# Full-height transposes of the half-height attention tiles, and a larger constant in the planner's matmul time

## The chip, the core and the metric

One core of a Trainium2 chip runs the kernel. The metric is the device time of one execution in microseconds (us), taken as the median of several runs. Names of engines are those of the profile: PE is the matrix engine (TensorE), PEld its weight loads, DVE the vector engine, ACT the scalar engine, POOL GpSimd, and SP the queue from which the DMAs are issued.

## What is computed

Attention with a forget gate for 4 batches of 8 heads, 576 rows and 64 columns each, and then two MLPs on its 2304 rows of 512 values, with 2048 hidden units each. All is float32.

```python
scores = scale * np.matmul(q, k.transpose(0, 1, 3, 2))
cum = np.cumsum(np.log(np.clip(f, 0.0001, 1.0)), axis=-1)
scores = np.where(causal, -1e9, scores + cum[:, :, :, None] - cum[:, :, None, :])
attn = np.exp(scores - np.max(scores, axis=-1, keepdims=True))
attn = attn / (np.sum(attn, axis=-1, keepdims=True) + 1e-09)
x = rows(np.matmul(attn, v))               # (2304, 512)
h = x @ w_in;  x = np.maximum(0.01 * h, h) @ w_out
h = x @ w_in2; out = (np.maximum(h, 0.0) + alpha * np.minimum(h, 0.0)) @ w_out2
```

## The kernel before

**Work and stages.** A float32 operand of most products is carried as two float32r parts, hi and lo, and a product is three products of parts. The two MLPs go over 9 blocks of `T` = 256 rows each. A block of the first MLP is 16 chunks of 128 hidden units: `moe_h` multiplies into a chunk (L522, 12 matmuls of 256 columns) and `moe1_y` out of it (L591, 12 of 256 columns). The second MLP does the same with L522 and, in `moe2_y`, L642 (6 matmuls of 512 columns a chunk). The weights come as float64 and are rebuilt on ACT, POOL and DVE while the first block of each MLP runs; some of the first MLP's are then streamed from DRAM for each block (`ws`).

**Attention** is laid out in eight groups, group 0 and group 1 of each batch in turn (`ORDER`). A group 0 holds query rows 0 to 319, a group 1 rows 320 to 575. Every group is done head by head, and a head in query windows of 128 rows (`UNITS`). Group 0 has three windows, which start at rows 0, 128 and 192; of the last only the lower 64 rows count, since the upper 64 belong to the window before (`nq` = 64, `p0 = P - nq` = 64). Scores (L881, with a mask by L886 for the first heads) go to a PSUM bank, DVE adds the decay (L895), ACT takes the exponential (L906), DVE adds and inverts the row sum (L762, L767), and L921 or L923 multiplies the row tile `t` by it. Then `attention_weights` transposes `t` key tile by key tile on PE (L938) into the PSUM tile `tp`, ACT or DVE copies that into `pt` as the hi part (L361 or L363, called from `p_hi`), and DVE subtracts for the lo part (`p_lo`, L952). The product with v is L785 for the first two groups, whose operands stay float32 (`native`), and L795 for the others.

For the window with 64 rows, L938 reads rows 64 to 127 of `t` alone, against the 64x64 lower corner of the identity, and writes 64 columns for each of its three key tiles. All other windows are transposed with 128 rows against the whole identity.

**The order of the work** on all engines is written out ahead by `Plan.run`, a list scheduler that works when the kernel is built. Each operation comes with an engine (or several to choose from), an expected time and a due time; each engine takes the one that is due first among those whose operands and ring slots are free. DMAs are one such engine. The expected time of a matmul is `t_mm(n)` = `max(n / 2.4 + 2.5, 109)` ns for `n` columns, and that of a float32 product of four passes is `t_mm4(n)`. [...] `t_mm` also sets the due times: `span` of a block is 16 chunks x 24 products x `t_mm(256)`, plus 15 us (`ATT_NS`) while attention is left, except that the first block has 60 us. A group's attention is due from `LEAD` = 10 us ahead of a block on; the activations of a chunk are due 8 us (`URGENT`) and the streamed weights 10 us (`AHEAD`) before the product that needs them. On the chip the engines follow the order of the plan, and wait on semaphores for each other, not for the planned times.

Of the kernel before, what the change touches and what calls it, by code (L numbers as in the profile page):

```python
# [62 lines left out]
class Buf:  # L63
    """One tile of a ring; it is allocated when its first operation is emitted."""
# [7 lines left out]
class Ring:  # L72
    """Slots for tiles of a kind, taken in the order of the program, or by whoever comes first."""

    def __init__(self, bufs, make, after=None, ordered=True):
        self.make, self.after, self.ordered = make, after, ordered
        self.made = self.taken = 0
        self.free = [(0, None, i) for i in range(bufs)]  # when and by which engine a slot was left
# [9 lines left out]
class Plan:  # L88
    """List scheduling: operations are given with engine, expected time, due
    time and the buffers they touch; each engine takes the one that is due  # L90
    first among those whose operands and slots are there. They are emitted in
    the order of their start."""
# [4 lines left out]
    @staticmethod  # L97
    def latency(a, b):
        """Expected time between the end of an operation and its user's start."""
        if "dma" in (a, b):  # L100
            return 1000 * (a == "dma") + 1250 * (b == "dma")
        return (0 if a == "pe" else 125) if a == b else 260 if b == "pe" else 200 if a == "pe" else 170

    def op(self, times, due, fn, r=(), w=(), a=(), after=(), hold=(), shared=False, busy=1.0):
        """times: engine -> ns for the engines that may take it, the usual one first; r: read,
        w: written, a: written in a part of its own, hold: only allocated, shared: whether DVE
        takes the SBUF ports that it shares with GpSimd, busy: how busy the PE is with it."""
# [19 lines left out]
    def run(self):  # L127
# [11 lines left out]
        ports = 0  # when the ports that DVE and GpSimd share are free  # L139

        def slots(o, eng, now):
            """When the slots that o has to take are there, or None."""
# [14 lines left out]
        def cost(o, eng, now):  # L157
            """When o would be done on an engine, with a price on the shared ports."""
# [9 lines left out]
        def better(o, eng, now):  # L168
            """Whether no other engine is a better place for o."""
# [13 lines left out]
        while events:  # L183
# [7 lines left out]
            for eng, queue in queues.items():  # L191
                if free.get(eng, 0) > now:
                    continue
                for n in [n for _, n in queue]:
# [17 lines left out]
                    if eng == "pe":  # L212
                        # the array's clock is halved after a tick with few columns
# [31 lines left out]
# Expected times in ns for n columns.  # L245
def t_mm(n, passes=1):
    return passes * max(n / 2.4 + 2.5, 109)
# [43 lines left out]
def tile_forgetting_attention_two_moe(ctx: ExitStack, tc, qk0, qk1, v0, v1, fg, w1, w2, alphaT, out):  # L291
    """Causal softmax attention with a forget-gate decay, then two leaky MLPs.

    Every float32 operand of a matrix product is carried as two float32r parts
    of 12 significant bits, hi + lo, whose sum is exactly the operand.
    """
# [7 lines left out]
    # Each chunk of weights, 128 hidden units, comes in two halves: into and out  # L304
    # of them. Some halves of the first MLP's stay on chip, the others are kept
    # in DRAM once they are converted; some of the second's are converted ahead
    # and kept there too.
# [5 lines left out]
    # ---------------------------------------------------------------- groups  # L313
    # Query windows of 128 rows: (first row, rows that count from the end,
    # first key whose decay comes from the masked copy, key tiles). Key tiles
    # are windows of 128 keys too; where they overlap, v has zeros once.
    # Each group: queries, key tiles with the query they count from, and the
    # row whose cum is the origin of the decay.
# [17 lines left out]
    # Due times in ns: the first MLP's blocks of T rows follow the prologue, and  # L336
    # each group's attention is due during the block before the one it belongs to.
# [10 lines left out]
    # ----------------------------------------------------------------- pools  # L348
# [30 lines left out]
    # PSUM: some banks hold the blocks' outputs.  # L379
# [37 lines left out]
    # what the plan has to know of them  # L417
# [4 lines left out]
    # ------------------------------------------------------------- weights  # L422
    # The weights come as float64: pairs of words, the low one first. The high
    # word taken as a float32 and scaled by 2**-112 has its exponent rebased for
    # float32 (what underflows there becomes zero); shifted by three bits, with
    # the sign put back and the low word's top bits behind, it is the weight.
    w_t = {}

    def slot(which, f, half):
        """The second MLP's weights first take what is new on chip, then what the first leaves."""  # L430
# [8 lines left out]
    def weight(which, f, halves, d):  # L439
        """Load a part of a chunk of an MLP's weights and split it, due at d."""  # L440
# [58 lines left out]
    # ----------------------------------------------------------------- moe  # L499
# [8 lines left out]
    def moe_h(bi, f0, hp=None):  # L508
        """Two chunks of hidden units, which share a bank: product, leaky maximum, split."""
# [70 lines left out]
    def moe1_y(bi, f, g, acc):  # L580
        """Two of the four outputs share a bank, which the first product of the first opens."""
# [51 lines left out]
    def moe2_y(bi, f, g, acc):  # L633
# [17 lines left out]
        if f == NF - 1:  # L651
            parts = 2 if bi == 2 * NB - 1 else 1
            m = DM // parts
            for t in range(T // P):
                osb = new("ysb")
                for c in range(0, DM, m):
# [5 lines left out]
                    for grp in groups:  # L662
                        # the rows of the tile that belong to the group
# [13 lines left out]
    # ----------------------------------------------------------- attention  # L677
    x_raw = {}

    def attention_head(gi, h, d, span):  # L680
        """One head's rows of a group; its units are due from d on over span."""
# [38 lines left out]
        if gi == 0 and h < NBC:  # L720
            # the first heads' sums are broadcast by a product, which is there sooner
# [22 lines left out]
        def pt_ap(s, j0, j1, q0, q1):  # L744
            """Part s of the transposed weights of key tiles j0 to j1. The tiles lie one after
            the other; a last one that only the second window sees has no room for the first."""
# [34 lines left out]
        def pv_native():  # L781
            # v stands beside zeros, so that two heads' products are added in place
# [7 lines left out]
        # The two halves of the product's rows, v's hi and lo parts, are added.  # L790
# [13 lines left out]
        # the blocks that the group's rows belong to: block's tile, its columns, the group's  # L804
# [43 lines left out]
    # The scores are kept negated, without the rows' own cum_i, which cancels in  # L848
    # the softmax; what is added is cum_j less the cum of a row of the group.
# [64 lines left out]
    def attention_weights(g, u, d, t, nm, pt, pt_ap, native):  # L914
# [16 lines left out]
        for j0 in range(0, nb, step):  # L931
# [3 lines left out]
            def transpose(j0=j0, j1=j1, tp=tp):  # L935
                for j in range(j0, j1):
                    k0 = g["kt"][j][0]
                    pe.transpose(tp.ap[:, (j - j0) * nq : (j - j0 + 1) * nq], t.ap[p0:, k0 : k0 + P], ident[p0:, p0:])  # L938

            def parts_of(j0, j1, tp):  # L940
                src = tp.ap[:, : (j1 - j0) * nq]
                if j1 > j0 + 1:
                    src = src.rearrange("p (j q) -> p j q", q=nq)
# [12 lines left out]
            on("pe", (j1 - j0) * (nq / 1.2 + 2), d, transpose, r=[t, ident_b], w=[tp], hold=[pt], busy=nq / 256)  # L956
# [4 lines left out]
    # ------------------------------------------------------------ program  # L961
# [7 lines left out]
    # running sums of the log gates, less those of each group's origin, in two parts  # L969
# [7 lines left out]
    # brings the logarithm's table in  # L977
# [149 lines left out]
```

## Time and profile before

| | |
|---|---|
| time, median of 3 runs | 1046.72 us (1044.7 to 1049.14) |
| span of the profiled execution | 1043.5 us |
| PE busy | 1024.1 us, 98% |
| DVE, ACT, POOL busy | 651.7, 603.6, 85.9 us |
| DMA moved | 166.50 MB |

The time of the profiled execution is not listed apart from the three runs. Its span, from the first to the last instruction, is 3.2 us below their median. A busy time is a union of instructions that overlap in a pipeline, so PE's 98% does not say how fast it works while it is busy; for that one reads the starts of neighbouring groups in the timeline. The first MLP and the attention end at about 640 us, the second MLP fills the rest.

### The profile page before, as it was taken

What the parts mean: (1) busy time and instruction counts of PE and PEld (TensorE: products, weight loads), DVE (VectorE), ACT (ScalarE), POOL (GpSimd) and SP (SyncE); (2) the same over time, 40 slices, a digit from 0 to 9 for tenths busy, and PEclk for the clock granted to TensorE, in tenths of its full rate; (3) what the DMA queues carried; (4) which work ended last, traced back from release to release, by engine and by line L of the source; (5) the groups of instructions that cost most, each with busy time, mean ns of one, the idle gap of its engine ahead of it and who ended that gap; (6) DMA issues with size and microseconds to landing.
All of it is one profiled execution on the core that took longest, in us unless ns stands there. A gap on an engine that the chain in (4) does not pass through costs nothing.

```text
span 1043.5 us, 20123 instructions
## 1 busy us (share of the span) xinstructions
PE 1024.1 (98%) x7466; PEld 964.6 (92%) x7466; DVE 651.7 (62%) x1837; ACT 603.6 (58%) x1354; POOL 85.9 (8%) x159
## 2 busy tenths in 40 slices
PE   7899999999999999999999999999999999999998
PEld 5698999999999999999999999999999999999997
DVE  7799898888887877788885689423222322322322
ACT  7878787767787877887753456334333323323333
POOL 2000221210121111112010001000000000000000
PEclk9999999999999999999999999999999999999999
DMA  8899898576575665767489783001010100000000
GB/s 268 306 311 325 299 308 290 182 255 222 161 257 190 239 217 166 231 229 235 150 280 321 233 311 102 9 33 41 2 41 1 41 21 21 21 2 21 1 21 21
DMA packets 63234, 166.50 MB, mean 160 GB/s; under 512 B 6592, under 2 KB 20320, under 8 KB 63136
## 3 DMA queue, kind: packets, MB, share of 16 engines
q1 hardware_dynamic: 63136, 165.21, 47.2%
q8 instruction: 59, 0.97, 0.4%
q14 instruction: 39, 0.32, 0.1%
HBM read 148.29 MB, written 16.89 MB: 158 GB/s over the span
## 4 chain that ended last, share of the span: by engine, by line
PE 91%; DMA 6%; DVE 2%; ACT 1%; issue 0%; SPq 0%; ACTq 0%; DVEq 0%
PE bank L522 37%; PE bank L642 19%; PE bank L591 18%; PE bank L881 6%; PE bank L938 5%; PE bank L795 4%; PE bank L785 2%; DMA qk<-qk 2%; DMA vr<-v 1%; DMA ws<-wscr 1%; DMA yraw<-yd 1%; DMA raw<-w 1%; DVE g L366 0%; DVE t L895 0%; DVE cv L469 0%
## 5 line engine op out<-in xcount | busy, mean ns | idle before, releaser
L522 PE MATMUL bank<-x,w 128*128 128x256 f32 x1944 | 257.3, 284 | 0.1
L522 PEld LDWEIGHTS bank<-x,w 128*128 128x128 f32 x1944 | 243.7, 191 | 3.6 <-issue 0.4
L546 DVE SCALAR_TENSOR_TENSOR gr<-gr,nalpha,bank 128x256 f32<-128x256 f32 x144 | 62.8, 477 | 213.1 <-ACT bank L539 213.1
L361 ACT ACTIVATE g<-gr 128x512 fp32r<-128x512 f32 x143 | 90.1, 630 | 86.1 <-DVE gr L546 73.9
L366 DVE TENSOR_TENSOR g<-gr,g 128x512 fp32r<-128x512 f32 x144 | 100.6, 699 | 54.3 <-ACT g L361 53.9
L522 PE MATMUL bank<-x,ws 128*128 128x256 f32 x972 | 132.3, 285 | 1.2 <-DMA ws<-wscr 1.2
L536 ACT ACTIVATE gr<-bank 128x512 f32<-128x512 f32 x72 | 43.1, 598 | 154.7 <-PE bank L522 153.8
L642 PE MATMUL bank<-w,g 128*128 128x512 f32 x540 | 132.1, 391 | 0.0
L522 PEld LDWEIGHTS bank<-x,ws 128*128 128x128 f32 x972 | 123.5, 191 | 3.6 <-DMA ws<-wscr 1.7
L591 PE MATMUL bank<-g,ws 128*128 128x256 f32 x864 | 121.7, 288 | 1.3 <-ACT g L361 1.0
L591 PE MATMUL bank<-g,w 128*128 128x256 f32 x864 | 119.7, 286 | 0.0
L642 PEld LDWEIGHTS bank<-w,g 128*128 128x128 f32 x540 | 99.2, 188 | 19.4
L591 PEld LDWEIGHTS bank<-g,ws 128*128 128x128 f32 x864 | 109.5, 191 | 2.8 <-ACT g L361 1.4
L591 PEld LDWEIGHTS bank<-g,w 128*128 128x128 f32 x864 | 109.1, 191 | 0.4 <-issue 0.2
L906 ACT ACTIVATE t<-t,nm 128x128 f32<-128x128 f32 (+4 forms) x160 | 92.6, 580 | 17.2 <-DVE nm L895 16.6
L921 ACT ACTIVATE t<-t,nm 128x128 f32<-128x128 f32 (+4 forms) x139 | 78.2, 574 | 18.9 <-DVE nm L767 17.5
L858 POOL TENSOR_SCALAR_AFFINE_SELECT dm<-cb 128x128 f32<-128x128 f32 (+2 forms) x120 | 59.3, 496 | 358.3 <-DVE nm L895 274.9
L361 ACT ACTIVATE pt<-bank 128x128 fp32r<-128x128 f32 (+4 forms) x189 | 72.0, 408 | 25.9 <-PE bank L938 24.4
L938 PE MATMUL bank<-ident,t 128*128 128x128 f32 (+1 forms) x480 | 73.5, 269 | 1.5 <-ACT t L921 1.3
L952 DVE TENSOR_TENSOR pt<-bank,pt 128x128 fp32r<-128x128 f32 (+1 forms) x144 | 62.4, 452 | 11.7 <-ACT pt L361 10.3
L522 PE MATMUL bank<-x,v 128*128 128x256 f32 x540 | 69.6, 283 | 0.0
L522 PEld LDWEIGHTS bank<-x,v 128*128 128x128 f32 x540 | 68.1, 192 | 1.5
(98 smaller groups left out, 1407.6 us busy)
## 6 DMA issues: line engine op xcount, KB each, us to landing
ws<-wscr SPq DMA_DIRECT2D x112, 512.0 KB, 4.5
raw<-w SPq DMA_DIRECT2D x64, 512.0 KB, 6.3
qk<-qk SPq DMA_DIRECT2D x32, 416.0 KB, 4.4
qk<-qk SPq DMA_DIRECT2D x32, 320.0 KB, 4.5
cb<-cum_d SPq DMA_DIRECT2D x32, 288.0 KB, 4.4
vr<-v SPq DMA_DIRECT2D x16, 480.0 KB, 4.9
wscr<-ws SPq DMA_DIRECT2D x14, 512.0 KB, 5.7
cb<-cum_d SPq DMA_DIRECT2D x31, 160.0 KB, 4.2
```

The lines of the kernel that those rows point to most:

```text
L361: act.activation(out=out, in_=in_, func=AF.Copy)
L366: (dve if e == "dve" else gps).tensor_tensor(out=out, in0=in0, in1=in1, op=ALU.subtract)
L522: pe.matmul(h()[:, f - f0], lhsT=w.ap[:, a, c * P : (c + 1) * P], rhs=x.ap[:, s, c], start=c == 0 and i == 0, stop=c == NC - 1 and i == 2,)
L546: dve.scalar_tensor_tensor(out=gr.ap[:, i], in0=gr.ap[:, i], scalar=nalpha[:, f0 + i : f0 + i + 1], in1=h()[:, i], op0=ALU.mult, op1=ALU.add,)
L591: pe.matmul(acc[c // 2].ap[:, c % 2 * T :][:, :T], lhsT=w.ap[:, a, col : col + P], rhs=g.ap[:, s, at : at + T], start=f == 0 and (a, s) == ...
L642: pe.matmul(acc[t].ap, lhsT=g.ap[:, s, at + t * P : at + (t + 1) * P], rhs=w.ap[:, a], start=f == 0 and (a, s) == (0, 0), stop=f == NF - 1 ...
L858: gps.affine_select(out=dm.ap[:, : nk - split], in_=cb.ap[:, split:nk], pattern=[[-1, nk - split]], compare_op=ALU.is_ge, fill=-MASKED / S ...
L881: pe.matmul(sp_.ap[:, : s1 - s0], lhsT=q.ap[:, ql : ql + P], rhs=k, start=j == 0, stop=j == len(ks) - 1 and not masked,)
L906: act.activation(out=t.ap[:, :nk], in_=t.ap[:, :nk], func=AF.Exp, scale=-1.0, bias=nm.ap[:, last, u : u + 1], accum_out=nm.ap[:, 2, u : u ...
L921: act.activation(out=t.ap[:, :nk], in_=t.ap[:, :nk], func=AF.Copy, scale=nm.ap[:, 3, u : u + 1])
L938: pe.transpose(tp.ap[:, (j - j0) * nq : (j - j0 + 1) * nq], t.ap[p0:, k0 : k0 + P], ident[p0:, p0:])
L952: dve.tensor_tensor(out=lo, in0=src, in1=f32(hi), op=ALU.subtract)
```

## The change

Three lines of the transposes and one of the planner change. The half-height window is transposed like the others, with all 128 rows of `t` and the whole identity, into 128 columns for each key tile; what is copied out of `tp` is the last 64 columns of each. The planner's time for a transpose follows (`P / 1.2 + 2` in place of `nq / 1.2 + 2`, and `busy=0.5`). In `t_mm` the constant is 13.5 ns in place of 2.5 ns, with which all due times after the first block move too. The rest of the diff takes comments out and leaves out a `memset` of zero rows, of which there is none at these sizes.

```diff
 def t_mm(n, passes=1):
-    return passes * max(n / 2.4 + 2.5, 109)
+    return passes * max(n / 2.4 + 13.5, 109)
@@ attention_weights
-                    pe.transpose(tp.ap[:, (j - j0) * nq : (j - j0 + 1) * nq], t.ap[p0:, k0 : k0 + P], ident[p0:, p0:])
+                    pe.transpose(tp.ap[:, (j - j0) * P : (j - j0 + 1) * P], t.ap[:, k0 : k0 + P], ident)
 
             def parts_of(j0, j1, tp):
-                src = tp.ap[:, : (j1 - j0) * nq]
+                src = tp.ap[:, : (j1 - j0) * P]
                 if j1 > j0 + 1:
-                    src = src.rearrange("p (j q) -> p j q", q=nq)
+                    src = src.rearrange("p (j q) -> p j q", q=P)[:, :, p0:]
                 return src, [pt_ap(s, j0, j1, ql + p0, ql + P) for s in range(2)]
@@
-            on("pe", (j1 - j0) * (nq / 1.2 + 2), d, transpose, r=[t, ident_b], w=[tp], hold=[pt], busy=nq / 256)
+            on("pe", (j1 - j0) * (P / 1.2 + 2), d, transpose, r=[t, ident_b], w=[tp], hold=[pt], busy=0.5)
@@
-        on("pool", 100, -9.4e3, lambda i=i, rows=rows: gps.memset(rate[:rows, i : i + 1], -2.0 / SCALE), w=[rate_b])
+        if rows:
+            on("pool", 100, -9.4e3, lambda i=i, rows=rows: gps.memset(rate[:rows, i : i + 1], -2.0 / SCALE), w=[rate_b])
```

## Rows read from the trace of the kernel before

**Rows 1.** The page, part 1: busy us, share of the span, instructions.

```profile
PE 1024.1 (98%) x7466; PEld 964.6 (92%) x7466; DVE 651.7 (62%) x1837; ACT 603.6 (58%) x1354; POOL 85.9 (8%) x159
```

**Rows 2.** The page, part 4: the chain of work that ended last, by engine.

```profile
PE 91%; DMA 6%; DVE 2%; ACT 1%; issue 0%; SPq 0%; ACTq 0%; DVEq 0%
```

**Rows 3.** Windows by stage: length, busy us (instructions) by engine, clock, DMA share.

```profile
0.00:25.00 25.00, 18.99 (x80) 13.88 (x80) 18.17 (x77) 19.07 (x59) 6.66 (x17) 0.93 0.83 269
25.00:125.00 100.00, 94.19 (x635) 83.65 (x636) 89.37 (x265) 80.32 (x191) 6.93 (x10) 1.00 0.92 313
125.00:550.00 425.00, 423.87 (x3487) 416.79 (x3486) 352.65 (x1143) 323.21 (x787) 69.33 (x130) 1.00 0.68 227
550.00:640.00 90.00, 88.03 (x728) 87.22 (x727) 61.58 (x107) 42.66 (x75) 3.00 (x2) 1.00 0.73 254
640.00:1043.50 403.50, 399.00 (x2544) 363.11 (x2542) 129.95 (x250) 138.38 (x246) 0.00 (x0) 1.00 0.07 23
```

**Rows 4.** Groups by form, PE: the two shapes of L938 over the whole span.

```profile
L938 PE MATMUL bank<-ident,t 128*128 128x128 f32 x384 | 60.9, 275 | 1.1 <-ACT t L921 0.9
L938 PE MATMUL bank<-ident,t 64*128 64x64 f32 x96 | 12.9, 242 | 0.4 <-ACT t L921 0.4
```

**Rows 5.** Timeline of PE, a 64-row window: start us, length us, count.

```profile
165.50 1.12 PE L591 MATMUL bank<-g,ws 128*128 128x256 f32 x8
166.55 0.40 PE L938 MATMUL bank<-ident,t 64*128 64x64 f32 x3
166.88 0.74 PE L591 MATMUL bank<-g,ws 128*128 128x256 f32 x4
167.46 1.12 PE L591 MATMUL bank<-g,w 128*128 128x256 f32 x8
```

**Rows 6.** Timeline of PEld, the weight loads of the same stretch.

```profile
165.87 0.55 PEld L591 LDWEIGHTS bank<-g,ws 128*128 128x128 f32 x4
166.55 0.26 PEld L938 LDWEIGHTS bank<-ident,t 64*128 64x128 f32 x3
166.88 0.53 PEld L591 LDWEIGHTS bank<-g,ws 128*128 128x128 f32 x4
```

**Rows 7.** Timeline of PE, three transposes of 128 rows.

```profile
289.82 1.12 PE L591 MATMUL bank<-g,ws 128*128 128x256 f32 x8
290.78 0.49 PE L938 MATMUL bank<-ident,t 128*128 128x128 f32 x3
291.02 1.68 PE L591 MATMUL bank<-g,ws 128*128 128x256 f32 x12
292.54 0.22 PE L881 MATMUL bank<-k,k 128*128 128x128 f32 x1
```

**Rows 8.** Timeline of PE in the second MLP.

```profile
901.62 1.60 PE L522 MATMUL bank<-x,v 128*128 128x256 f32 x12
903.06 1.55 PE L642 MATMUL bank<-ws,g 128*128 128x512 f32 x6
904.44 1.52 PE L642 MATMUL bank<-w,g 128*128 128x512 f32 x6
905.80 4.48 PE L522 MATMUL bank<-x,v 128*128 128x256 f32 x36
```

**Rows 9.** Groups by form, PE, 0 to 60 us: the 64-row transposes.

```profile
L938 PE MATMUL bank<-ident,t 64*128 64x64 f32 x24 | 3.4, 250 | 0.0
```

**Rows 10.** Chain of waits, 0 to 60 us, merged pieces around one window and later.

```profile
32.80 5.22 DMA qk<-qk
...
38.68 0.34 PE bank L938 x3
39.06 0.20 issue
39.27 0.56 ACT t L921
39.84 0.42 DVE t L895
40.27 0.60 DVE cv L469
...
51.51 4.66 DMA vr<-v
```

**Rows 11.** PE's own waits, 0 to 125 us: total us, times, longest.

```profile
PE bank L881 <- DMA qk<-qk: 7.3, 4, 4.4
PE bank L785 <- DMA vr<-v: 2.5, 3, 1.4
```

**Rows 12.** Groups by form: the 192-column copies and subtractions out of PSUM.

```profile
L361 ACT ACTIVATE pt<-bank 128x192 fp32r<-128x192 f32 x24 | 7.9, 330 | 6.4 <-PE bank L938 6.1
L952 DVE TENSOR_TENSOR pt<-bank,pt 128x192 fp32r<-128x192 f32 x24 | 8.5, 353 | 2.8 <-ACT pt L361 2.7
```

**Rows 13.** PE's own waits, 125 to 640 us.

```profile
PE bank L522 <- DMA ws<-wscr: 1.2, 2, 0.9
PE bank L591 <- ACT g L361: 1.0, 2, 0.6
PE bank L938 <- ACT t L921: 0.4, 1, 0.4
PE bank L591 <- DVE g L366: 0.3, 1, 0.3
```

## The prediction

> **What bounds the kernel now.** I read the busy times first [rows 1]: PE is busy for 98% of the span, and nothing else for more than 62%. The chain of work that ended last says the same, 91% of it is PE [rows 2]. Busy is not the same as fast, so next come the windows by stage, for where PE is idle [rows 3]: 6.0 us in the first 25 us (25.00 less 18.99), 5.8 us up to 125 us, 1.1 us of the 425 us up to 550, 2.0 us around the change of the MLPs up to 640, and 4.5 us after it, most of it the tail. The granted clock is 1.00 of 2.4 GHz from 25 us on. So from about 60 us to the end PE is the bound: what is taken off PE's instruction stream there comes off the time one for one, as long as the other engines follow. DVE (352.65 us of 425) and ACT (323.21 us) have 17% and 24% to spare in the longest stage that has attention in it. In the first 60 us it is not PE: the chain changes there between late loads of 4.7 to 5.2 us, DVE and ACT [rows 10], and DMA is busy at 0.83 and 0.92 [rows 3].
>
> How fast PE goes is read from neighbouring starts in the timeline. Twelve products of 256 columns start over 1.44 us (901.62 to 903.06), 120 ns each, and twelve of 512 columns over 2.74 us, 228 ns each [rows 8]. Against 256 / 2.4 = 106.7 ns and 213.3 ns a product has a constant part of 13 to 15 ns.
>
> **The transposes, the part with a price.** There are 96 of 64 rows [rows 4], three for each of the 32 heads' windows of group 0. Take one window amid products that cost 120 ns each. From 165.50 to 167.46 us, 1.96 us, PE does twelve products of L591 and the three transposes [rows 5]: 1.96 - 12 x 0.120 = 0.52 us for the transposes. Where three transposes of 128 rows stand between the same kind of products, from 289.82 to 292.54 us, it does twenty products and the three in 2.72 us [rows 7]: 2.72 - 20 x 0.120 = 0.32 us, or 0.107 us each. The higher transposes are the cheaper ones, by 0.20 us a window; I read 0.19, as starts are rounded to 0.01 us and two are subtracted.
>
> Why this is so can be seen in the loads. The eighth product before the small transposes begins at 165.50 + 7 x 0.12 = 166.34, and the next instruction should begin at 166.46; the first small transpose begins at 166.55. The loads of the products before are all done by 166.42, yet the weight load of the first small transpose begins only with it, at 166.55, and the load of the first product behind them only with that product, at 166.88 [rows 5, 6]. So before the small transposes PE runs empty and loads nothing ahead, 0.09 us, and behind them it does so again. Before the transposes of 128 rows nothing of that is seen: eight products of 0.12 us from 289.82 end at 290.78, where the first transpose begins [rows 7].
>
> The sum: 24 of the 32 windows lie between 125 and 550 us (96 transposes in all [rows 4], 24 of them, eight windows, before 60 us [rows 9]). 24 x 0.19 = 4.6 us, all on the path. The eight early windows have 8 x 0.19 = 1.5 us. One of them is seen on the chain, at 38.68, but what follows it is ACT and then DVE, up to the next late load [rows 10]; PE has gaps there. I count half, 0.7 us, with 0 and 1.5 as ends. Together -5.3 us (-4.6 to -6.1).
>
> **What else the transposes touch costs nothing.** The identity has 128 columns, so each output has 128; three of them are 384 columns and fit the bank. Copy and subtraction still read 192 columns, now with a stride of 128: 330 ns on ACT and 353 ns on DVE today [rows 12]. No row shows the strided read. If it cost half as much again, 24 x (0.17 + 0.18) = 8 us would fall on two engines that have 102 and 72 us to spare in the same 425 us [rows 3]; PE's work hides it. That cover is missing only before 60 us, for eight windows of 0.17 us or 1.4 us at the most. The rows of `t` that are read in addition are written in any case, and no wait is added.
>
> **The planner.** No instruction is added or removed by the constant; it moves the order on all engines and the choice between ACT, DVE and POOL. `t_mm(256)` goes from 109.2 to 120.2 ns and `t_mm(512)` from 215.8 to 226.8, against the 120 and 228 ns of the trace [rows 8]. So the plan had PE 9% too fast in the MLPs and now has it right. The spans of the due times grow from 41.9 to 46.1 us (384 products) plus 15 us. The fixed leads of 10, 10 and 8 us thus become a slightly smaller part of a block. The DMA queue of SP moves with it, all its loads.
>
> The Trainium skill (TensorE: Matmul & The Clock Gate, section Back-to-back issue gap) speaks against this part: it gives N/2.4 + 2.5 ns for the gap, the constant of before. By that page the plan would now be 10% off, by the trace it comes into step; the time of the products on the chip is the same either way, so it bears only on the chances of the two rivals about the order below, and there I go by the trace's 120 ns.
>
> What the new order is worth no row of before shows. It can't win more than PE's idle time that isn't the start or the tail: 5.8 + 1.1 + 2.0 = 8.9 us [rows 3]. Its steady part has nothing to win: of 425 us PE lacks 1.1 us, and all its own waits up to 640 us are 2.9 us in seven pieces [rows 13]. What it can lose is bounded by the nearest rows, late loads before 60 us, at 0.6 to 2 us of PE for a common one (7.3 us in four, 2.5 us in three) and 4.4 us for the worst [rows 11]. I take 0: between a plan that is nearer to the truth and a new order in a stage whose DMA is at 0.92, I see no sign. The ends are -4 us (about half of what is idle) and +7 us (several such loads).
>
> **The sum.** -5.3 us against the span of 1043.5 gives 1038.2 us. The span is 3.2 us below the median of the runs; with that kept, 1046.7 - 5.3 = 1041.4 us. This lies at the edge of the 0.5% (5.2 us, about what a measurement of this kernel can tell from no change), so faster and same split the forecast's chance.
>
> **The rivals.**
> - The order gains too: with PE's times right, loads and conversions before 125 us and at the change of the MLPs come in the order in which PE wants them. Half of 5.8 + 2.0 us, 3.9 us, is won: 1037.5 us. For it: the waits there are for single loads [rows 11, 13]. Against it: DMA is at 0.92 of its time, so a load put earlier puts another one later. 0.22.
> - The order loses a part: one more late load of 4.4 us [rows 11] at the start, 1045.8 us. 0.17.
> - The order loses much, slower than before. The place is the first 125 us. The plan now has PE slower there, so it puts loads of the first weights and of `qk` and `vr` in another order on SP's one queue; every load that is issued behind a wait for a buffer comes late, and PE, which follows a fixed order, stands still. Price: a late load on the chain is 4.7 to 5.2 us [rows 10]. The second such load makes up for the transposes, the third makes it slower: 1041.4 + 3 x 5.2 = 1057 us. 0.08.
> - The transposes don't gain what I say: the gaps around the small ones belong to their place in the program (a wait for `t`) and not to their height. Then the gaps stay and the columns double. By the rows a column of a transpose is 0.107 / 128 us, so 64 more in each of 96 cost at most 96 x 0.053 = 5.1 us: 1051.8 us, still within 0.5%. The same page of the Trainium skill (Back-to-back issue gap) lets the gap grow with the columns, some 60 cycles at 64 and 134 at 128; by it alone, an estimate, 96 x 31 ns = 3.0 us would be added. Against it: transposes of 128 rows wait for the same `t` and show no gap [rows 7]. 0.03.
>
> **How the numbers follow.** The forecast has 0.50, with 1039 to 1044 as its own range; 0.28 of it is below 1041.5, 0.22 above. Faster: 0.28 + 0.22 = 0.50. Same: 0.22 + 0.17 + 0.03 = 0.42. Slower: 0.08. The range reaches down to the gain of order with a little more, 1036 us (-5.3, -4 and 1 us of scatter), and up to the sum with +7 us, 1048.5.
>
> **What would show it.** In the profile after, no 64x64 form of L938 is left and there are 480 of 128x128; twelve to twenty products around three transposes again leave 0.32 us in the timeline; PE's weight loads run ahead into the transposes; PE's busy time from 125 to 550 us becomes shorter for the same work, so that the last L795 comes some 4 us earlier relative to the first. Idle time of PE before 125 us still near 12 us means that the order did nothing; 7 us or less is the first rival, 20 us or more the third. The prediction is wrong if the windows of group 0 don't become shorter by 0.19 us each, or if the first 125 us change by more than the transposes give.

## The result, and the profile after

The changed kernel is slower: 1056.4 us against 1045.7 us (medians of four runs each), a ratio of 1.0099 (95% interval 1.0079 to 1.0120). The forecast was 1041.4 us. Below, "tall" and "small" stand for transposes of 128 and of 64 rows.

The page of the changed kernel, parts 1 and 4 (answers to [rows 1, 2]):

```profile
PE 1027.1 (97%) x7466; PEld 967.1 (92%) x7466; DVE 659.3 (62%) x1842; ACT 603.2 (57%) x1360; POOL 81.2 (8%) x148
...
PE 79%; DVE 8%; DMA 7%; ACT 4%; issue 2%; POOL 0%; ACTq 0%; SPq 0%; DVEq 0%
PE bank L522 33%; PE bank L642 19%; PE bank L591 15%; PE bank L881 4%; PE bank L938 4%; PE bank L795 3%; DMA raw<-w 3%; DMA vr<-v 3%; PE bank L785 2%; DVE g L366 1%; DVE t L895 1%; ACT t L906 1%; DVE pt L952 1%; DVE cv L463 1%; DVE gr L542 1%
```

PE is as busy as before, but only 79% of the chain that ended last is PE, against 91% [rows 2]. DVE has 8% of it where it had 2%, ACT 4% where it had 1%, and loads of raw weights (`raw`) stand on it with 3%. The windows by stage, with the columns of [rows 3], show where:

```profile
0.00:25.00 25.00, 19.40 (x80) 14.50 (x80) 17.75 (x74) 18.48 (x56) 5.77 (x16) 0.93 0.83 267
25.00:125.00 100.00, 90.97 (x611) 80.08 (x610) 89.50 (x261) 78.11 (x188) 4.84 (x7) 1.00 0.91 306
125.00:550.00 425.00, 420.96 (x3437) 413.38 (x3436) 352.24 (x1141) 320.27 (x790) 66.87 (x123) 1.00 0.69 223
550.00:640.00 90.00, 85.50 (x710) 85.07 (x709) 62.04 (x109) 41.04 (x71) 0.76 (x1) 1.00 0.80 275
```

From 25 to 125 us PE begins 611 matmuls where it began 635, from 125 to 550 us 3437 in place of 3487, and 710 in place of 728 after that. The granted clock of these stages is as before. The transposes did what was forecast; groups by form of the changed kernel (answers to [rows 4, 12]):

```profile
L938 PE MATMUL bank<-ident,t 128*128 128x128 f32 x480 | 76.9, 277 | 2.1 <-DVE t L923 1.3 <-ACT t L921 0.4
...
L361 ACT ACTIVATE pt<-bank 128x192 fp32r<-128x192 f32 x24 | 7.8, 325 | 1.1 <-PE bank L938 1.1
...
L952 DVE TENSOR_TENSOR pt<-bank,pt 128x192 fp32r<-128x192 f32 x24 | 8.4, 349 | 0.0
```

All 480 are tall, and the copies and subtractions that now read with a stride take 325 and 349 ns, where they took 330 and 353.

### The profile page after: what moved, and what is told of

Same layout as the page of the kernel before. It is cut to its first block, busy times and chain, and to the rows that moved or that the text cites. A ratio compares the mean times of both kernels' runs of the same rounds, so it can differ in the third digit from the quotient of the medians.

```text
span 1055.0 us, 20133 instructions
## 1 busy us (share of the span) xinstructions
PE 1027.1 (97%) x7466; PEld 967.1 (92%) x7466; DVE 659.3 (62%) x1842; ACT 603.2 (57%) x1360; POOL 81.2 (8%) x148
## 4 chain that ended last, share of the span: by engine, by line
PE 79%; DVE 8%; DMA 7%; ACT 4%; issue 2%; POOL 0%; ACTq 0%; SPq 0%; DVEq 0%
PE bank L522 33%; PE bank L642 19%; PE bank L591 15%; PE bank L881 4%; PE bank L938 4%; PE bank L795 3%; DMA raw<-w 3%; DMA vr<-v 3%; PE bank L785 2%; DVE g L366 1%; DVE t L895 1%; ACT t L906 1%; DVE pt L952 1%; DVE cv L463 1%; DVE gr L542 1%
## 5 line engine op out<-in xcount | busy, mean ns | idle before, releaser
L361 ACT ACTIVATE g<-gr 128x512 fp32r<-128x512 f32 x142 | 89.4, 630 | 96.7 <-DVE gr L546 75.1
L522 PE MATMUL bank<-x,ws 128*128 128x256 f32 x972 | 129.7, 284 | 0.0
L591 PE MATMUL bank<-g,w 128*128 128x256 f32 x864 | 120.2, 288 | 3.5 <-ACT g L361 3.3
L591 PE MATMUL bank<-g,ws 128*128 128x256 f32 x864 | 120.0, 288 | 3.7 <-ACT g L361 3.3
L591 PEld LDWEIGHTS bank<-g,ws 128*128 128x128 f32 x864 | 109.2, 191 | 5.9 <-ACT g L361 4.8
L591 PEld LDWEIGHTS bank<-g,w 128*128 128x128 f32 x864 | 108.9, 191 | 5.4 <-ACT g L361 4.7
L906 ACT ACTIVATE t<-t,nm 128x128 f32<-128x128 f32 (+4 forms) x160 | 92.5, 579 | 27.2 <-DVE nm L895 26.7
L361 ACT ACTIVATE pt<-bank 128x192 fp32r<-128x192 f32 (+4 forms) x189 | 71.0, 404 | 22.9 <-PE bank L938 22.1
L938 PE MATMUL bank<-ident,t 128*128 128x128 f32 x480 | 76.9, 277 | 2.1 <-DVE t L923 1.3
L921 ACT ACTIVATE t<-t,nm 128x128 f32<-128x128 f32 (+4 forms) x127 | 69.1, 557 | 12.5 <-DVE nm L767 9.1
L642 PE MATMUL bank<-v,g 128*128 128x512 f32 x270 | 66.5, 392 | 0.0
```

Of the source, the lines that this page charges most:

```text
L361: act.activation(out=out, in_=in_, func=AF.Copy)
L522: pe.matmul(h()[:, f - f0], lhsT=w.ap[:, a, c * P : (c + 1) * P], rhs=x.ap[:, s, c], start=c == 0 and i == 0, stop=c == NC - 1 and i == 2,)
L591: pe.matmul(acc[c // 2].ap[:, c % 2 * T :][:, :T], lhsT=w.ap[:, a, col : col + P], rhs=g.ap[:, s, at : at + T], start=f == 0 and (a, s) == ...
L642: pe.matmul(acc[t].ap, lhsT=g.ap[:, s, at + t * P : at + (t + 1) * P], rhs=w.ap[:, a], start=f == 0 and (a, s) == (0, 0), stop=f == NF - 1 ...
L906: act.activation(out=t.ap[:, :nk], in_=t.ap[:, :nk], func=AF.Exp, scale=-1.0, bias=nm.ap[:, last, u : u + 1], accum_out=nm.ap[:, 2, u : u ...
L921: act.activation(out=t.ap[:, :nk], in_=t.ap[:, :nk], func=AF.Copy, scale=nm.ap[:, 3, u : u + 1])
```

## The experiments

Each kernel is compared with the kernel before on the same chip. "The planner" is what writes the order of all engines; a kernel whose planner is told other times does the same work, in another order and with some of the shared operations on another of ACT, DVE and POOL.

Two questions were put first: whether the transposes or the new order cost the time (theories A and B), and then what it is in the order. Theory S: with PE's true time the plan leaves PE no slack, and what the other engines and the loads are late by is waited for. Theory U: the due times do it. Theory D: every new order is a fresh draw, and the old one was a lucky one.

For a stage's loss I use one measure throughout. Each matmul of PE gets the time to the next one's start, less a fixed price of its shape that comes from undisturbed starts (n / 2.4 + 13.3 ns for the MLPs' products, 109 ns for a tall transpose, and so on); the sums over a stage are **PE's lost time**. The prices are the same for all kernels and hold at the full clock of 2.4 GHz, so differences count, not the sums, and work at the lower clock counts as lost too. Each row is one execution, up to 3.3 us off the median beside it. (The profiled execution of e2 took 1070.3 us, so no stages are given for it.) The stages are 0 to 60 us (start), 60 to 150, 150 to 500 (steady), 500 to 670 us (change from the first MLP to the second); as the kernels run up to some 20 us apart, a stage does not hold quite the same work in each.

| kernel | time us | ratio (95%) | 0-60 | 60-150 | 150-500 | 500-670 |
|---|---|---|---|---|---|---|
| before (small) | 1044 to 1046 | | 15.2 | 3.3 | 13.1 | 4.5 |
| changed kernel | 1056.4 | 1.0099 (1.0079 to 1.0120) | 18.9 | 5.6 | 13.8 | 10.0 |
| e1 tall, old order | 1039.8 | 0.9960 (0.9945 to 0.9975) | 13.9 | 3.1 | 9.7 | 3.3 |
| e2 small, new order | 1061.5 | 1.0164 (1.0147 to 1.0181) | | | | |
| e3 tall alone | 1045.3 | 1.0011 (0.9993 to 1.0028) | 19.3 | 4.6 | 10.0 | 4.4 |
| e4 constant alone (small) | 1063.8 | 1.0190 (1.0174 to 1.0205) | 14.9 | 7.6 | 20.1 | 11.1 |
| e5 PE's times alone | 1067.0 | 1.0196 (1.0167 to 1.0225) | 18.5 | 6.0 | 20.4 | 9.2 |
| e6 due times alone | 1045.3 | 0.9998 (0.9979 to 1.0017) | 19.3 | 5.2 | 10.4 | 2.7 |
| e7 constant of 8 ns | 1053.0 | 1.0067 (1.0041 to 1.0094) | 17.4 | 2.2 | 16.7 | 5.5 |
| e8 true loads | 1054.8 | 1.0085 (1.0056 to 1.0114) | 22.5 | 3.6 | 16.1 | 3.3 |
| e9 others planned slower | 1059.2 | 1.0132 (1.0091 to 1.0173) | 21.1 | 8.7 | 10.0 | 9.9 |
| e10 others planned faster | 1057.2 | 1.0116 (1.0096 to 1.0136) | 18.0 | 5.1 | 16.1 | 9.0 |
| e11 PE planned faster | 1051.8 | 1.0067 (1.0049 to 1.0085) | 22.4 | 7.8 | 11.6 | 0.8 |
| e12 late operands | 1071.7 | 1.0250 (1.0225 to 1.0276) | 25.0 | 10.5 | 20.4 | 7.9 |
| e13 constant after 140 us | 1052.8 | 1.0096 (1.0068 to 1.0124) | 14.3 | 3.1 | 14.2 | 10.6 |
| e14 PE faster after 140 us | 1037.1 | 0.9930 (0.9915 to 0.9945) | 14.8 | 2.9 | 8.5 | 2.3 |
| e15 slack after 140 us | 1037.0 | 0.9933 (0.9918 to 0.9947) | 14.6 | 3.2 | 8.8 | 0.5 |

### The transposes against the order (e1, e2)

```diff
# e1: as the changed kernel on the chip, but the planner is told what it was told before
-    return passes * max(n / 2.4 + 13.5, 109)
+    return passes * max(n / 2.4 + 2.5, 109)
-            on("pe", (j1 - j0) * (P / 1.2 + 2), d, transpose, ..., busy=0.5)
+            on("pe", (j1 - j0) * (nq / 1.2 + 2), d, transpose, ..., busy=nq / 256)
# e2: the planner as in the changed kernel, but pe.transpose and parts_of as before
```

> The 128-row transposes on the chip, but the planner is told the old times (constant 2.5 ns, 64-row transposes), so every engine keeps the order of the kernel before. Theory A (the order costs, the transposes gain): 32 windows x 0.19 us less on PE, 4.6 to 6.1 us below before, 1039.6 to 1041.1 against 1045.7. Theory B (the transposes themselves cost, by a strided read, by more columns or by drains that stay): at or above before, 1046 to 1057.

> The 64-row transposes of before on the chip, but the planner is told the new times, so every engine has the order of the changed kernel. Theory A: the changed kernel plus 4.6 to 6.1 us, 1061 to 1062.5 against its 1056.4. Theory B: below the changed kernel, toward 1046.

Measured: e1 1039.8 us, e2 1061.5 us. Every engine of e1 has the instructions of the kernel before in the same order, every engine of e2 those of the changed kernel. So the tall transposes gain 4.7 us under the old order (1044.5 - 1039.8) and 5.1 us under the new one (1061.5 - 1056.4); by the ratios of the table it is 4.2 and 6.8 us. That is theory A; theory B is out. The new order costs about 17 us under either kind (1056.4 - 1039.8 = 16.6, 1061.5 - 1044.5 = 17.0; by the ratios 14.5 and 17.1). This is the window of [rows 5] in e1, in the timeline of PE, and the weight loads of its transposes:

```profile
163.90 1.12 PE L591 MATMUL bank<-g,ws 128*128 128x256 f32 x8
164.85 0.49 PE L938 MATMUL bank<-ident,t 128*128 128x128 f32 x3
165.10 0.71 PE L591 MATMUL bank<-g,ws 128*128 128x256 f32 x4
165.65 1.11 PE L591 MATMUL bank<-g,w 128*128 128x256 f32 x8
...
164.75 0.35 PEld L938 LDWEIGHTS bank<-ident,t 128*128 128x128 f32 x3
```

The same twelve products and three transposes take from 163.90 to 165.65 us, 1.75 us, where they took 1.96: 0.21 us less. The transposes begin where the eighth product's 0.12 us end (163.90 + 0.96), with no gap, and their weight loads begin 0.10 us ahead of them. The Trainium skill (TensorEngine Tiling (Array Packing), section Tiling Modes) names what was removed: a change between a 64-row and a 128-row mode drains the engine. The trace agrees, and here it has a price, 0.09 us before the small transposes and 0.10 us behind: the four products from 166.88 to 167.46 us [rows 5] take 0.58 us where four take 0.48.

### Each half by itself (e3, e4)

```diff
# e3: the changed kernel with
-    return passes * max(n / 2.4 + 13.5, 109)
+    return passes * max(n / 2.4 + 2.5, 109)
# e4: the kernel before with
-    return passes * max(n / 2.4 + 2.5, 109)
+    return passes * max(n / 2.4 + 13.5, 109)
```

> The transposes with their own planned time, the constant left at 2.5 ns: the first half of the change alone. If the constant is what spoils the order, this is 1039 to 1042. If any new order costs, because the old one was a lucky draw, it is above 1046 although PE has 6 us less to do: 1046 to 1056.

> The constant of 13.5 ns alone, with the 64-row transposes on the chip and in the plan: the second half of the change. If the constant spoils the order: about 1061 (the changed kernel and the 5 us that the small transposes cost). If it is a matter of the draw: anywhere from 1046 to 1065, not near 1061 in particular.

Measured: 1045.3 and 1063.8 us. The constant alone costs 19 us. But e3 is no 1040 either: the planned time of the transposes alone moves the order as well, and with that 5 us are lost at the start (19.3 in place of 13.9). At the start the constant is not the cause: with it alone e4 keeps the order of the kernel before on all engines up to 53 us, and loses 14.9 us there, where the kernel before loses 15.2. Thus two things had to be told apart: what the planned time of the transposes does, and what the constant does.

### PE's times or the due times, and how much (e5, e6, e7)

```diff
# e5: changed kernel, due times as before
-        span.append(FIRST if i == 0 else NF * 6 * NC * t_mm(T) + (...))
+        span.append(FIRST if i == 0 else NF * 6 * NC * 109.1667 + (...))
# e6: e3 with due times as in the changed kernel
-        span.append(FIRST if i == 0 else NF * 6 * NC * t_mm(T) + (...))
+        span.append(FIRST if i == 0 else NF * 6 * NC * 120.1667 + (...))
# e7: changed kernel
-    return passes * max(n / 2.4 + 13.5, 109)
+    return passes * max(n / 2.4 + 8.0, 109)
```

> 128-row transposes, planned as such; the constant of 13.5 ns only in PE's expected times, the due times as with 2.5 ns. Theory S (with PE's true time the plan leaves PE no slack, so what other engines and DMAs are late by is waited for): as slow as the changed kernel, 1053 to 1059. Theory U (the due times, with leads that are a smaller part of a block, do it): near the tall transposes alone, 1045. Theory D (every new order is a fresh draw): anywhere from 1040 to 1062.

> 128-row transposes on the chip; PE's expected times as in the kernel before (2.5 ns, 64-row transposes), and only the spans of the due times worked out with 13.5 ns. Theory S: near the tall transposes under the old order, 1038 to 1045. Theory U: 1053 to 1059. Theory D: anywhere from 1040 to 1062.

> The changed kernel with a constant of 8 ns in place of 13.5. Theory S: between the tall transposes alone (1045, 2.5 ns) and the changed kernel (1056, 13.5 ns), 1048 to 1053. Theory D: no trend, as likely outside of these as between.

Measured: 1067.0, 1045.3 and 1053.0 us. The expectation of e6 says that its planner has the transposes with 64 rows. The kernel that ran has them with 128, as e3 has, so it is compared with e3: 1045.3 us both, and 19.3 us lost at the start in both. The due times alone cost nothing; PE's expected times carry the loss, and half of the step costs 7.7 of the 11.1 us between e3 and the changed kernel. e5 came out slower than any of the theories had it (S 1053 to 1059, D up to 1062): beside the constant the new due times, which it lacks, are worth 10.6 us (1067.0 - 1056.4). Why was not looked into. After 150 us the loss sorts itself by how PE is planned: 10 us in the steady stage and 3 to 4 at the change with 2.5 ns (e1, e3, e6), 14 to 20 and 6 to 10 with 8 or 13.5 ns (e7, the changed kernel, e5). Within the second three it does not follow the constant: 8 ns loses more in the steady stage (16.7) than 13.5 ns in the changed kernel (13.8). One sees it in the weight loads, which wait where a product's operands are late. Windows of 150 to 500 us (PE busy, then PEld busy), for e1, the changed kernel and e5:

```profile
150.00:500.00 350.00, 349.80 (x2906) 348.01 (x2905) 291.40 (x983) 271.84 (x673) 57.27 (x114) 1.00 0.68 222
```

```profile
150.00:500.00 350.00, 349.15 (x2870) 344.59 (x2870) 285.07 (x961) 263.02 (x659) 53.21 (x105) 1.00 0.69 218
```

```profile
150.00:500.00 350.00, 344.61 (x2816) 338.23 (x2816) 279.60 (x945) 269.29 (x663) 54.82 (x105) 1.00 0.66 215
```

PE's own busy share hides most of it (349.80 and 349.15); PEld is idle for 2.0, 5.4 and 11.8 us, and 36 and 90 matmuls fewer begin. At 0.12 us each the 36 are 4.3 us, the 4.1 us by which the lost times of e1 and the changed kernel differ. In e5 the largest wait of PEld in this stage is for the row tiles of the attention (waits of PEld: total us, times, longest), where e1 has 0.2 us:

```profile
PEld bank L938 <- ACT t L921: 6.8, 14, 1.7
```

### What is late at the change of the MLPs (e8)

Between 500 and 670 us the second MLP's weights are loaded and converted while the first MLP's last blocks run. This is the longest stall there, in the changed kernel's timeline of all engines:

```profile
560.79 2.56 PE L591 MATMUL bank<-g,ws 128*128 128x256 f32 x20
...
561.00 0.68 DVE L542 TENSOR_TENSOR gr<-bank,gr 128x512 f32<-128x512 f32 x1
...
564.87 0.66 ACT L453 ACTIVATE cv<-raw 128x512 f32<-128x512 f32 x1 [4.45 <-DMA raw<-w]
565.43 0.62 ACT L361 ACTIVATE g<-gr 128x512 fp32r<-128x512 f32 x1
...
566.10 1.58 PE L591 MATMUL bank<-g,ws 128*128 128x256 f32 x11 [2.75 <-ACT g L361]
```

DVE has finished the activation (`gr`) at 561.68. Its cast (`g`, L361) is a matter of 0.6 us on ACT, but ahead of it in ACT's fixed order stands the first step of a weight conversion (L453), whose raw weights are still on the way. ACT waits 4.45 us for the load with the cast behind it, and PE 2.75 us for the cast. On the chain of waits that load stands with 8.24 us:

```profile
556.61 8.24 DMA raw<-w
```

The plan has a load of 512 KB there 2.5 us after it is issued (512 KB at 360 bytes per ns, and 1000 ns); the page has 6.2 us for the median of `raw<-w`. The kernel before has the same fault, and ACT waits for raw weights there too, 7.4 us in this stage, but PE waits only 1.0 us for the cast. By theory S that is because PE was 9% too fast in its plan, so that what PE needs came first. e8 tells the planner how late loads land:

```diff
# e8: changed kernel
-            return 1000 * (a == "dma") + 1250 * (b == "dma")
+            return 3000 * (a == "dma") + 1250 * (b == "dma")
-    return max(nbytes / 360, 530)
+    return max(nbytes / 310, 530)
```

> The changed kernel, with the planner told how late loads land: 3000 ns in place of 1000 from the end of a transfer to its user, and 310 in place of 360 bytes per ns (the trace has 4.5 to 6.2 us from issue to landing of 512 KB, the plan 2.5 us, with this 4.7 us). Theory S, in the form that what comes late are loads, with ACT and PE behind them in fixed order: 1044 to 1050, and fewer waits of PE for the activations of a chunk. Theory D, or a cause other than the loads: 1051 or more.

Measured: 1054.8 us, so the time as a whole missed theory S and lies in the range of its rivals; but where the theory speaks of loads it holds. The lost time at the change of the MLPs falls from 10.0 to 3.3 us. ACT's wait for raw weights, 500 to 670 us, in the changed kernel and in e8 (total us, times, longest):

```profile
ACT cv L453 <- DMA raw<-w: 13.5, 6, 4.4
```

```profile
ACT cv L453 <- DMA raw<-w: 1.1, 2, 0.7
```

and PE's wait for the cast in the same stage, in the two:

```profile
PE bank L591 <- ACT g L361: 6.0, 4, 2.8
```

```profile
PE bank L591 <- ACT g L361: 0.4, 1, 0.4
```

The steady stage did not gain (16.1, where the changed kernel loses 13.8), and the start became worse by 3.6 us.

Late loads by themselves do not cost PE time, though. In e14 below, where PE is planned too fast, ACT waits longer for raw weights at the change than in the changed kernel, and PE hardly waits for the cast (500 to 670 us, e14):

```profile
ACT cv L453 <- DMA raw<-w: 15.9, 13, 6.7
```

```profile
PE bank L591 <- ACT g L361: 0.4, 1, 0.4
```

By these traces a late load costs PE time only where work that PE needs stands right behind it on ACT.

### PE against the other engines in the plan (e9 to e12)

```diff
# e9 (1.1) and e10 (0.91, with the constant of 2.5 ns), in Plan.op
+        times = {e: t * (1.1 if e in ("dve", "act", "pool") else 1) for e, t in times.items()}
# e11
-    return passes * max(n / 2.4 + 13.5, 109)
+    return passes * max(n / 2.4 - 8.5, 98)
# e12, in Plan.latency
-  260 if b == "pe"
+  760 if b == "pe"
```

> The changed kernel, with every expected time of ACT, DVE and POOL times 1.1; PE keeps its true time. What counts in theory S is how fast PE is in the plan against the others, and that is back to what it was with 2.5 ns: 1044 to 1050, PE's lost time between 150 and 500 us about 10 us (13.8 in the changed kernel). If only PE's own planned time matters: 1053 to 1060.

> The tall transposes with the constant of 2.5 ns, and every expected time of ACT, DVE and POOL times 0.91: the same ratio to PE as in the changed kernel, but with the old constant. Theory S: 1050 to 1060, PE's lost time between 150 and 500 us 14 to 20 us in place of 10. If the constant itself matters: near the tall transposes alone, 1042 to 1048.

> The changed kernel with n / 2.4 - 8.5 ns and a floor of 98 ns: the plan has PE 18% too fast. Theory S: more slack than with 2.5 ns, 1040 to 1046, lost time between 150 and 500 us at most 10 us. If instead the old constant was a lucky draw and any other is worse: 1050 to 1060.

> The changed kernel, with the expected latency from another engine to PE 760 ns in place of 260: PE's operands are planned to be there half a us early, its own time stays true. Theory S, if half a us is enough slack: 1043 to 1050. If the slack that is missing is longer than that (late loads of several us): 1051 to 1058.

Measured: 1059.2, 1057.2, 1051.8 and 1071.7 us. Of the times only e10 came as theory S had it; e9 and e11 lie in the ranges of their rivals, and e12 outside of both of its ranges. The steady stage went by theory S in the first two: PE's true time with slower planned engines loses 10.0 us there, the old constant with faster planned ones 16.1. e11 loses 11.6 there, a little more than was set (10), and 0.8 at the change of the MLPs. Up to 3.4 us of the 11.6 are the clock's, half of the 6.8 us in which it stood at 1.2 GHz in e11:

```profile
149.90:156.70 6.80, 6.27 (x28) 5.69 (x27) 6.45 (x18) 4.66 (x11) 0.42 (x1) 0.50 1.01 327
```

What spoils e9 and e11 are the start (21.1 and 22.4 us) and 60 to 150 us (8.7 and 7.8), and in e9 also the change of the MLPs, where its loads are as late as in the changed kernel. e12 failed outright: half a us more of planned latency gives no slack (20.4 in the steady stage). Why it became as slow as that was not looked into, and theory S as it stands does not say it.

### The start taken out (e13, e14, e15)

The start differs by up to 11 us and hides the rest. The traces say what it goes by. Up to 53 us the kernel before, e1, e4 and the three of this section have one order on all engines, and lose 13.9 to 15.2 us at the start; the planner of each has the early transposes with 64 rows. The changed kernel, e3, e5, e6 and e7 have one other order up to 60 us, with constants of 2.5, 8 and 13.5 ns among them, and lose 17.4 to 19.3; their planners have the transposes with 128 rows, 108.7 ns in place of 55.3 (`P / 1.2 + 2` and `nq / 1.2 + 2`). e8 to e12 have the transposes so too, and each an order of its own (18.0 to 25.0). So the start went with the planned time of the transposes and not with the constant. Part of it is the clock: it fell to 1.2 GHz for a while in the first 60 us of some kernels. Windows of 0 to 60 us, e4, e3 and e11:

```profile
0.00:60.00 60.00, 49.05 (x267) 38.25 (x268) 47.92 (x189) 47.82 (x141) 9.11 (x21) 1.00 0.91 301
```

```profile
0.00:60.00 60.00, 45.81 (x236) 35.90 (x236) 48.25 (x189) 48.07 (x142) 7.81 (x19) 0.97 0.88 300
```

```profile
0.00:60.00 60.00, 46.52 (x214) 37.45 (x215) 41.26 (x172) 43.85 (x133) 5.93 (x17) 0.86 0.80 258
```

At 0.97, as in the changed kernel too, this is worth at most 1.8 us (0.03 x 60), and at 0.86 (e11 and e12) at most 8.4; PE had waited in e11 for late loads, 6.4 us for v and 4.2 us for q and k before 50 us.

So these three keep the old plan up to 140 us of planned time, and with it the order of the kernel before.

```diff
# all three: the planner's PE times are pairs, old and new (from 140 us on), and due times stay as before
+    ns = ns.real if now < 140e3 else ns.imag
# new times of PE: tall transposes, and n / 2.4 + 13.5 without a floor (e13, e15) or max(n / 2.4 - 8.5, 98) (e14)
# e15 also, from 140 us on
+    ns = o.times[eng] * {"pe": 1, "dma": 360 / 310}.get(eng, 1.1)
+    d.end + self.latency(d.eng, eng) + 2000 * (d.eng == "dma")
```

> Tall transposes; the plan works with the old times (2.5 ns, 64-row transposes, old due times) up to 140 us of its own time, so that the order up to there is that of the kernel before, and with PE's true times (13.5 ns) from there on. Theory S: PE's lost time as under the old order up to 150 us (17 us), 14 to 20 us between 150 and 500, 9 to 11 us between 500 and 670; 1037.7 of span grows by 10 to 17 us, 1049 to 1056 in time. If all of the loss came from the first 140 us: 1040 to 1043.

> The same cut at 140 us, with PE planned faster than it is from there on (n / 2.4 - 8.5 ns, floor 98). Theory S: 17 us lost up to 150 us, 10 to 12 us between 150 and 500, 1 to 3 us between 500 and 670; 1037 to 1041. If a new order costs in any case: 1045 to 1055.

> The same cut at 140 us; from there on PE has its true times (13.5 ns), but ACT, DVE and POOL are planned 1.1 times as long, transfers at 310 bytes per ns, and their landing 2 us later. Theory S, in full: the slack is back, though the constant is that of the changed kernel: 10 to 12 us lost between 150 and 500, 3 to 5 us between 500 and 670, 1038 to 1043. If a true PE time costs by itself: 1049 to 1056.

Measured: 1052.8, 1037.1 and 1037.0 us, the last a little below what was set, the others inside. The start is that of e1 in all three (14.3 to 14.8 us, granted clock 1.00), so PE's true times cost by themselves, 1052.8 - 1039.8 = 13 us after the start (11.3 between the profiled executions, with spans of 1049.0 and 1037.7 us). These times differ from those of the changed kernel in one thing: they have no floor of 109 ns for narrow products. And e15 has the same true time of PE and none of the loss. Windows of 150 to 500 us, e13 and e15:

```profile
150.00:500.00 350.00, 348.85 (x2868) 344.79 (x2867) 288.81 (x973) 273.67 (x672) 59.29 (x109) 1.00 0.69 221
```

```profile
150.00:500.00 350.00, 350.00 (x2914) 348.96 (x2912) 290.03 (x990) 267.14 (x662) 59.68 (x117) 1.00 0.71 223
```

PEld is idle for 5.2 us in e13 and for 1.0 in e15, and at the change of the MLPs e15 loses 0.5 us. e15 changes three planned times at once, and was not taken apart; e9 (other engines slower alone, 10.0 us in the steady stage, 9.9 at the change) and e8 (late loads alone, 16.1 and 3.3) suggest that the first serves the steady stage and the loads the change. Over all kernels, those planned with slack (e1, e3, e6, e9, e11, e14, e15) lose 8.5 to 11.6 us in the steady stage, the other tall ones 13.8 to 20.4, e12 among them. A fresh draw for every order (theory D) would hardly sort them so. e14 and e15 are faster than both kernels of this case and than e1.

## Why the prediction was wrong

- **What bounds the kernel**: right for the kernel before. The sentence that PE's gain comes off one for one "as long as the other engines follow" named the condition that fell.
- **The transposes**: right in mechanism and size. -5.3 us were forecast (-4.6 to -6.1), -4.7 and -5.1 were measured under the two orders, 0.21 us in the window of [rows 5] against 0.19. The early windows' half share was not measured apart. The signs named for it came: no 64x64 form, 480 of 128x128, 1.75 - 12 x 0.120 = 0.31 us for three transposes, and weight loads ahead of them. From the first to the last L795 it is 3.8 us less in e1 (133.1 to 513.0 us) than in the kernel before (134.1 to 517.8), as forecast; in the changed kernel it is 2.2 us more (140.3 to 526.2): there the new order cost more than the transposes gained.
- **What else they touch**: right. The strided reads cost nothing.
- **The planner**: the step that failed is "I take 0", with ends of -4 and +7 us. The new order costs 16.6 us (1056.4 - 1039.8). By lost time it is 5.0 us at the start, 2.5 from 60 to 150, 4.1 in the steady stage and 6.7 at the change of the MLPs, 18.3 in these four (the spans are 17.3 us apart). Two terms were missing. The planned time of the transposes was costed on the chip alone and not in the plan, where it moves the start: e3 loses 5.4 us more there than e1. And the bound of the loss was drawn from the waits that the kernel before has at its start [rows 11]. The rows of the rest show almost none [rows 13] (2.9 us in six pieces, not seven), and I read from that that the steady part had nothing to win. True; but it has much to lose: 10.8 of the 18.3 us were lost after 150 us. That PE does not wait there is the work of the order, whose cover is the 9% by which PE was planned too fast.
- **"A plan that is nearer to the truth"** was the wrong thing to weigh. PE's time became true, the loads' did not (2.5 us planned, 6.2 measured). My reading is that a plan in which PE is exact puts its operands there just in time, and each is late by what the plan leaves out. e8 and e14 show this for the loads at the change of the MLPs; e15 shows that slack takes away all of the loss from 140 us on. For the steady stage the single latenesses stay unnamed: only that slack cures them is shown.
- **The rivals**: that the transposes gain nothing is out by e1. The one that ends slower had the sign and a chance of 0.08. Its place, the first 125 us, holds 5.0 + 2.5 of the 18.3 us by lost time up to 150 us. Its mechanism, loads that are late on SP's queue, is seen there in part: PE's waits for v and for q and k from 0 to 150 us, in the changed kernel and in e1:

```profile
PE bank L785 <- DMA vr<-v: 6.0, 4, 2.9
PE bank L881 <- DMA qk<-qk: 5.5, 3, 4.3
```

```profile
PE bank L881 <- DMA qk<-qk: 7.4, 4, 4.7
PE bank L785 <- DMA vr<-v: 1.8, 2, 1.5
```

- Together they are 11.5 us in place of 9.2, so late loads are 2.3 of the 7.5 us. And the reason given, PE planned slower, holds for the transposes alone: e3 and e6 have the old constant in PE's other times and lose as much at the start (19.3 us each), and e4, with the new constant alone, does not (14.9). The order of the kernel before was the best start of all that were tried. Why it is better than the others stays open.
- **The rule of the Trainium skill** (TensorE: Matmul & The Clock Gate, Back-to-back issue gap) was weighed by asking which constant is true. The section gives N/2.4 + 2.5 for a product by itself, not for a stream of weight loads and products, which the prediction did not say. The trace's 120 ns still stand against it here. Yet the plan does better with the smaller number.
- **What would show it**: PE's idle time before 125 us is 5.6 + 9.0 = 14.6 us in the changed kernel, between the 12 of "did nothing" and the 20 of the third rival. That the first 125 us changed by more than the transposes give, named as a sign of being wrong, came true: 24 matmuls fewer begin there from 25 us on. For the stages after 125 us the one sign was the interval of L795; for the change of the MLPs, where the largest part was lost (6.7 us), there was none.

## What to carry to other kernels

Where the order of the work is written ahead by a planner, an error in one engine's time can be slack that the others live on; correcting it alone can be slower, so correct what comes late (loads, above all those that stand ahead of urgent work on an in-order engine) or plan for margin, in the same step. Before a new order is costed at nothing, ask what the old one covers in the stages that show no waits, and price a loss there too. Change one planned time in a run: here two were changed, and the one that seemed harmless, the transposes', cost 5 us at the start. And when an edit moves the whole order, compare it with the same edit under the old order: here that took apart a gain of 5 us and a loss of 17 us that one time had mixed.

## What was not expected of the hardware

The products of float32 operands are faster than the four passes a column that the planner has for them. In the kernel before's chain of waits, ten products of L785 of two heads (eight of 256 columns and two of 128) take

```profile
69.01 1.95 PE bank L785 x10
70.96 2.40 PE bank L591 x20
```

1.95 us for 2304 columns, 0.85 ns each, or two periods of the 2.4 GHz clock that is granted there; the products of L591 beside them take 2.40 / (20 x 256) = 0.47 ns a column. A planner with the right number there was not tried. And reading 64 of every 128 columns out of PSUM costs neither ACT nor DVE anything (325 and 349 ns for 192 columns).
